# A fused sliding-window attention and GeGLU block on one core: the copy of the negated row maxima is issued in a later slot, and the last phase's weight loads and result stores are issued by GpSimd

## The chip, the cores and the metric

The kernel runs on one core of one Trainium2 chip. The metric is device time in microseconds (us) of one execution; the time of a kernel is the median of several executions. A profiled execution has a time of its own, and a span, which is the part of it that the hardware profiler recorded from the first instruction to the last.

The engines are called as in the profile: PE is TensorE's matmul, PEld its weight load, DVE is VectorE, ACT is ScalarE, POOL is GpSimd, SP is SyncE, which here does nothing but issue DMAs. "SPq" and "ACTq" are the queues from which SP and ACT issue DMAs; an issue is a short entry of such a queue, and the transfer itself runs later on the core's 16 DMA engines. Each engine takes its instructions in the order of the program; an instruction that waits holds up all that are behind it on the same engine. "L537" is line 537 of the kernel.

## The reference

One layer for 2048 tokens of width 640. The output is `x + attention(layernorm(x)) + geglu(layernorm(x))`, all in float32:

```python
qkv = xn @ wqkv                       # 32 heads of width 20
scores = q @ k.T * 20 ** -0.5         # a token sees itself and the 255 before it
p = softmax(where(0 <= i - j < 256, scores, -1e9))
attention = (p @ v) @ wo
geglu = (gelu(xn @ w_gate) * (xn @ w_up)) @ w_down      # inner width 1728
```

## The kernel before

**Number formats.** The dense products need more precision than one fast pass gives, so each float32 operand is split into a high part (a rounded copy, made by ACT) and a low part (the remainder, made by DVE or GpSimd), and each product is three matmuls: high by high, low by high, high by low. For the scores, q and k are split into three bf16 parts that are stacked along the partition axis, so that one matmul sums the products of parts.

**Stages.** Norm, transposes and the first projections come first (to about 102 us). Attention follows (102 to 541 us), with the remaining q, k and v projections and the first part of gate/up as filling for TensorE. Then the rest of gate/up (541 to 801 us), and last the down projection together with the attention's output projection (801 to 1041 us), which this text calls the last phase.

**Attention.** The work is cut into 32 units, u = 0 to 31; a unit is a group of 4 heads and a chunk of 512 tokens. `attention()` (L818) writes out the order of every engine's instructions by hand. A unit has a period of `NS` = 14 slots, and in each slot the loop puts down what is due: actions that were queued earlier for this slot (`at(slot, fn)`, `defer(n, fn)`, run by `tick()` at the start of a slot; those given to `late` are put down by `flush()` later in the same slot), then the fixed pieces, then dense matmuls as filling (`pull_fill`, 30.9 / 14 of them in each slot). In a period these matter here:

- *Stack loads.* `load_stack(u + 3)` brings q and k of a later unit from DRAM (qd, kd) into the stacked buffers qs and ks, by six DMAs each. SP issues the six of ks at the end of slot 9 (`KSLOT`) and the six of qs at the end of slot 12 (L473 to L482). There are several buffers of each, used in turn.
- *Row maxima.* In some slots `max_pair` makes scores of a later unit by matmul (L507) and DVE takes the maximum of each row (L517). The maxima are negated and, in slot 7 (`MXD`), `max_end(u)` (L531 to L537) turns them into rows: a matmul with the identity (L534), a copy by ACT into a small tile `mr` (L536), and a DMA issued by ACT (L537) that writes `mr` into rows 60 and 61 of the stacked buffer qs of unit u. That is "the row of negated maxima". The unit's score matmuls read these rows along with q, so that the maximum is subtracted inside the matmul.
- *Exponentials.* In the odd slots up to 11 of the unit's own period, which is the one after, `exp_piece` (L558) makes two banks of scores by matmul (L572) and ACT takes the exponential (L574). The first of these matmuls, in slot 1, is the first reader of the row. GpSimd masks the edges (L587, L590).
- *Outputs.* In slot 0 of the next period `av_unit` multiplies the exponentials by v (L615) and ACT copies the two results out (L621, L622); GpSimd adds them in slot 3, and SP stores them in slot 6 (L629, L630).
- *Projections.* `save_qk` splits a finished projection into the three bf16 parts `pt`, by ACT (L255), DVE and GpSimd (L259), and SP stores them to qd or kd (L268). Weights come by L234 and, for gate/up, by loads that ACT issues at some times.

All of SP's DMAs are one queue, in the order written. A DMA on one of the hardware queues also counts on one of a small set of completion semaphores, which the program's builder hands out in turn to SP's and ACT's DMAs alike; a DMA waits for the earlier one on its semaphore, even when that is one of another engine. So an issue can have to wait for a transfer that has nothing to do with its data.

**Last phase.** There are 80 steps: 8 passes p over 256 tokens each, and a pass has 9 steps of a quad of the inner width (two times 128 rows of the weight) and a tenth for the rest. In each step n of the loop:

- `load_step(n + 4)`: SP loads the activations of a step that is four later, into one of 5 buffers `hr`.
- `split_step(n + 2)`: ACT makes high parts (L1198), DVE low parts (L1077).
- `prepare(n)`: work on the weights, by the table `plan` (L1425): "f" fetches a quad's float32 weights into one of three staging buffers `stg` (`fetch`, L1031 to L1047, the DMA in L1043), "h" makes its high part on ACT (L1058), "l" its low part on DVE (L1062 and L1077), "s" forms sums of it on DVE. "b4" is the weight of quad 4, "t4" the sums of the same quad; the nine fetches in the table are b7, b8, t6, t8, t7, t0, t1, t2 and t3, in this order, in steps 4 to 12. They are issued by ACT (`eng=nc.scalar` in L1434). A fetch waits until its staging buffer has been read for the last time.
- `terms` (L1244): the matmuls, 128 x 320 each.
- `drain(p)` (L1262 to L1315), after a pass: DVE adds the accumulators into the tile `xr`, which holds x, and `store` (L1269 to L1271) writes its two halves to the output; SP issues these stores. `get_x` (L1317) loads x for the next pass into `xr`, in the fourth step of that pass.

After the table's fetches the weights are all in place, and the later passes only load activations.

Of the kernel before, what the change touches and what calls it, by code (L numbers as in the profile page):

```python
# [28 lines left out]
SR = 3 * DH  # L29
QROWS = 64 + SR  # L30
NS = 14
# [2 lines left out]
V1_SLOT = 169  # L34
MXD = 7
KSLOT = 9
LAG = 3, 5, 4, 4, 4, 4, 3, 3, 4, 3, 2, 1, 1, 1
NFA = 3
HD = D // 2
# [28 lines left out]
def block_kernel(ctx, tc, x, wqk, wv, wgu, wdo, wdl, out):  # L68
    nc = tc.nc
# [128 lines left out]
    now = [None]  # L198

    def at(slot, fn, *a):  # L200
        acts.setdefault(slot, []).append((fn, a))
# [3 lines left out]
    def late(fn, *a):  # L205
        if now[0] is None or now[0] < NS:
            fn(*a)
        else:
            lates.append((fn, a))

    def flush():
        while lates:
            fn, a = lates.pop(0)
            fn(*a)

    def lag():
        return 1 if now[0] is None or now[0] < NS else LAG[now[0] % NS]

# [119 lines left out]
    NQ, NK = 3, 4  # L338
    qs = [st1.tile([128, 4, C], BF, name=f"qs{i}") for i in range(NQ)]
# [133 lines left out]
    def load_stack(u, which=(0, 1)):  # L473
        g, c = divmod(u, NC)
        for m in range(80 * g // 128, (80 * g + 79) // 128 + 1):
            assert all((m + 5 * i, c) in done for i in which), (u, m)

        for i in which:
            dst, src, top, again = ((qs[u % NQ], qd[c], 1, 2), (ks[u % NK], kd[c], 0, 0))[i]
            for j in (0, 2):  # L480
                for p, part, n in ((j * 32, top, 2), (j * 32 + 2 * DH, again, 1), (64 - j * 32, 0, 3)):
                    nc.sync.dma_start(dst[p:p + DH * n, j:j + 2].rearrange("p j t -> p (j t)"),  # L482
                                      src[g, part:part + n].rearrange("s (d j) t -> (s d) (j t)",
                                                                      j=4)[:, j * C:(j + 2) * C])
# [46 lines left out]
    def max_end(u):  # L531
        nm = maxes.pop(u)
        ps = psm.tile([128, 128], F32, name="ps_n", tag="mx")
        nc.tensor.matmul(ps, nm.rearrange("p z a j b -> p (z a j b)"), identb, start=True, stop=True)  # L534
        mr = ap.tile([32, 128], BF, name="mr", tag="mr")
        nc.scalar.activation(mr, ps[0:32], AF.Copy)  # L536
        late(lambda: nc.scalar.dma_start(qs[u % NQ][SR:SR + 2].rearrange("p j t -> p (j t)"), mr))  # L537

    def pieces(c):
        b = 4 * c  # L540
# [259 lines left out]
    def pull_max(n, slot):  # L800
        for _ in range(n):
            x = next(stream, None)
            if x is None:
                return
            max_pair(*x)
            if x[1] == 7:
                at(slot + (MXD if slot >= 0 else 4), max_end, x[0])

    def tick():
        todo = [y for t in sorted(t for t in acts if t <= now[0]) for y in acts.pop(t)]  # L810
        return sorted(todo, key=lambda y: y[0] is max_end)

    def pull_fill(n):
        debt[0] += n
        while debt[0] > 0:
            debt[0] -= next(fill, 1.0)

    def attention():  # L818
# [22 lines left out]
        for u in range(NU + 1):  # L841
            for i in range(NS):
# [17 lines left out]
                flush()  # L860
                if u + 3 < NU and i in (KSLOT, 12):
                    load_stack(u + 3, (int(i == KSLOT),))
                pull_fill(RATE / NS)
# [164 lines left out]
    def four(t):  # L1028
        return t.rearrange("p k (h n) -> p (k h) n", h=2)

    def fetch(kind, q, where="stg", eng=nc.sync):  # L1031
        if where == "wr":
            ts = [wrp.tile([128, KT, 128], F32, name="wr", tag="wr").rearrange("p k m -> p (k m)") for _ in range(2)]
        elif where != "stg" and where != "at":
            ts = [tp.tile([128, D], F32, name=f"b{n}{q}", tag=f"x{n}{where}") for n in "hl"]
        if where != "stg" and where != "at":
            for i, t in enumerate(ts):
                nc.sync.dma_start(t, wdo[q][:, i])
            staged[kind, q] = [(t.rearrange("p (h n) -> p h n", h=2), slice(2 * i, 2 * i + 2)) for i, t in enumerate(ts)]
            return  # L1040
        pool, bufs = (rp3, 3) if where == "stg" else (cp, 3)
        t = pool.tile([128, 4, HD], F32, name="stg", tag=where, bufs=bufs)
        eng.dma_start(t, four(wdo[q]) if kind == "b" else wtd[q])  # L1043
        if kind == "t" and q in borrow:
            staged[kind, q] = [(t[:, i:i + 1], slice(i, i + 1)) for i in range(4)]
        else:
            staged[kind, q] = [(t, slice(0, 4))]  # L1047

    def parts(kind, q):
        for raw, dst in staged[kind, q]:  # L1050
            if kind == "t" and q in borrow:
                yield raw, quads["b", borrow[q] + dst.start], slice(1, 2)
            else:
                yield raw, slots(kind, q)[0][0], dst
# [15 lines left out]
    def sum_quad(q):  # L1070
        (t, _), = staged["b", q]
        for fn in sum_items(t):
            fn()
        staged["t", q] = [(t[:, i:i + 1], slice(i, i + 1)) for i in range(4)] if q in borrow else [(t, slice(0, 4))]

    def sub(o, i, j, op=OP.subtract):
        nc.vector.tensor_tensor(out=o, in0=i, in1=j, op=op)  # L1077
# [65 lines left out]
    NP = S // 256  # L1143
# [118 lines left out]
    def drain(p, ps, xt):  # L1262
        xs = {(r, h): xt[:, 2 - r, h * HD - HD:h * HD] for r in (1, 2) for h in (1, 2)}
        rows = {1: slice(256 * p + 128, 256 * p + 256), 2: slice(256 * p, 256 * p + 128)}

        def add(r, h, i, eng=nc.vector):
            eng.tensor_tensor(out=xs[r, h], in0=i, in1=xs[r, h], op=OP.add)  # L1267

        def store(r, h=None):  # L1269
            cs = slice(h * HD - HD, h * HD) if h else slice(0, D)  # L1270
            nc.sync.dma_start(out[rows[r], cs], xt[:, 2 - r, cs])  # L1271

        b = {i: ps[i][:, 0:HD] for i in ps}
        if p == 0:
            for bank, r, h in ((2, 1, 1), (3, 1, 2), (4, 2, 1), (8, 2, 2)):
                add(r, h, b[bank])
                if h == 2:
                    store(r)
            return
        a = copies.pop(p)  # L1280
        both = cp.tile([128, 2, HD], F32, name="u2", tag="r13")
        q, c5 = both[:, 0], both[:, 1]
        if p < NP - 1:
            nc.scalar.activation(c5, b[5], AF.Copy)
        if p == NP - 1:
            add(1, 1, b[2])
            add(1, 1, a)
            store(1, 1)
            sub(q, b[6], a, OP.add)
            add(1, 2, q)  # L1290
            sub(q, b[7], q, OP.add)
            add(2, 1, q)
            add(2, 2, q)
            add(2, 1, b[4])
            store(2, 1)
            add(1, 2, b[5])
            add(2, 2, b[5])
            store(2, 2)
            add(1, 2, b[3])
            store(1, 2)  # L1300
            return
        add(2, 1, b[4])
        sub(q, b[6], a, OP.add)
        add(1, 2, q)
        sub(q, b[7], q, OP.add)
        add(1, 2, b[3])
        add(1, 2, c5)
        add(1, 1, a)
        store(1)
        add(2, 1, q)  # L1310
        add(2, 2, c5)
        add(2, 2, q)
        if p == 1:
            add(2, 2, b[8])
        store(2)  # L1315
# [114 lines left out]
    def prepare(n):  # L1430
        for op in plan.get(n, "").split():
            kind, q = op[1], int(op[-1])
            if op[0] == "f":
                fetch(kind, q, eng=nc.scalar)  # L1434
            elif op[0] == "s":
                sum_quad(q)
            elif op[0] == "p":
                kind, q, i = "t", int(op[1]), int(op[2])
                for raw, t, dst in parts(kind, q):
                    raw, dst = (raw, dst) if q in borrow else (raw[:, i:i + 1], slice(i, i + 1))  # L1440
                    if q not in borrow or t is quads["b", borrow[q] + i]:
                        nc.scalar.activation(t[:, 0, dst], raw, AF.Copy)
                        sub(t[:, 1, dst], raw, t[:, 0, dst].bitcast(F32))
            else:
                (high_quad if op[0] == "h" else low_quad)(kind, q)
        if n == 2:
            nc.scalar.activation(w13[:, 0], raw13, AF.Copy)
            sub(w13[:, 1], raw13, w13[:, 0].bitcast(F32))
        if n == 0:
            fetch("b", 5)  # L1450
            fetch("b", 6)
# [76 lines left out]
```

## Time and profile before

| | |
|---|---|
| median of 3 executions | 1044.87 us (1044.46 to 1046.39) |
| the profiled execution | 1045.72 us |
| its span | 1044.0 us |
| instructions | 25563 |
| bytes moved by DMA | 158.74 MB, on average 152 GB/s |
| share of the 16 DMA engines' time, queue 1 (hardware) | 44.5% |

The span is 1.7 us shorter than the execution's own time; these lie around what is recorded.

How to read it: the page's first part gives for each engine its busy time, its share of the span and its number of instructions. The second part cuts the span into 40 slices of 26.1 us, with a digit for the busy share of each (9 is 90% or more):

```profile
ACT  4534766767666666666675322233224554433332
POOL 5122788888755787766461111101110000000000
...
DMA  5552356554633354343325576662216874433333
```

Counted from 0, slices 4 to 20 are attention: ACT and POOL are busiest there. From slice 31 on, which is the last phase, POOL has no work. There the DMA engines have their peak (8, then 7) in the slices that begin at 809 and 835 us, where the weights are fetched.

In the lists of groups, a row has the engine, the line, the operation and its tiles, a count and durations. In a timeline, a row is a start in us, a duration in us (for "x6" rows: from the first start to the last end of the six), the engine and the instruction, and in brackets how long the engine stood idle before it and which operation ended that. In a list of waits a row names the waiting line, what it waited for, and the total, number and longest of these waits.

### The profile page before, as it was taken

The numbers are of one execution on the slowest core, as the hardware profiler recorded it, in microseconds if no ns is written. First come the engines' busy times: TensorE is split into PE (matmuls) and PEld (weight loads), VectorE is DVE, ScalarE is ACT, GpSimd is POOL, SyncE is SP. The second block draws the span as 40 slices with busy tenths as digits, with TensorE's granted clock in tenths as the row PEclk, the third lists the DMA queues.
The fourth block names the chain that finished last, engine by engine and source line by source line (L and its number), as shares of the span: only waits on it lengthen the run. The fifth ranks groups of instructions, "written<-read, shape, count | busy, mean of one in ns | idle before, by whom it ended". The sixth has DMA issues, their size and how long they took to land.

```text
span 1044.0 us, 25563 instructions
## 1 busy us (share of the span) xinstructions
PE 1033.4 (99%) x9393; PEld 834.3 (80%) x9393; DVE 741.7 (71%) x2018; ACT 527.5 (51%) x1120; POOL 385.5 (37%) x623
## 2 busy tenths in 40 slices
PE   9999999999999999999999999999999999999998
PEld 8887666666777666666678888888888999999998
DVE  7755666677655676677736778776555889888887
ACT  4534766767666666666675322233224554433332
POOL 5122788888755787766461111101110000000000
PEclk9999999999999999999999999999999999999999
DMA  5552356554633354343325576662216874433333
GB/s 211 180 157 70 110 157 183 165 181 142 183 98 100 114 168 138 103 134 110 99 77 193 188 244 212 253 250 105 78 59 242 263 249 136 138 127 123 117 121 106
DMA packets 102150, 158.74 MB, mean 152 GB/s; under 512 B 14172, under 2 KB 55260, under 8 KB 102024
## 3 DMA queue, kind: packets, MB, share of 16 engines
q1 hardware_dynamic: 99640, 150.94, 44.5%
q10 hardware_dynamic: 2384, 6.16, 1.7%
q8 instruction: 74, 1.21, 0.5%
q14 instruction: 52, 0.43, 0.1%
HBM read 101.78 MB, written 54.92 MB: 150 GB/s over the span
## 4 chain that ended last, share of the span: by engine, by line
PE 90%; DVE 5%; ACT 2%; DMA 2%; issue 1%; POOL 0%; ACTq 0%; DVEq 0%; SPq 0%
PE ps_g L972 22%; PE ps_d L108 20%; PE ps L1244 20%; PE ps_e L572 8%; PE ps_v L108 7%; PE ps_o L615 5%; PE ps_m L507 5%; DVE junk L517 2%; PE ps_g L108 1%; DMA stg<-wdo 1%; ACT wb L1058 1%; PE ps_d L356 1%; PE ps_t L185 0%; DVE wb L1077 0%; DMA qs<-qd 0%
## 5 line engine op out<-in xcount | busy, mean ns | idle before, releaser
L517 DVE CUSTOM_DVE_ANT_0 junk<-ps_m,mask 128x320 bf16<-128x320 f32 (+2 forms) x512 | 243.0, 475 | 128.9 <-PE ps_m L507 71.0
L574 ACT ACTIVATE P<-ps_e 128x512 f32<-128x512 f32 (+2 forms) x384 | 198.7, 572 | 68.3 <-PE ps_e L572 67.8
L1244 PE MATMUL ps<-wb,at 128*128 128x320 f32 x999 | 156.4, 309 | 0.8 <-DVE xr L1267 0.8
L1244 PEld LDWEIGHTS ps<-wb,at 128*128 128x128 f32 x999 | 148.9, 188 | 1.5 <-issue 1.0
L587 POOL TENSOR_SCALAR_AFFINE_SELECT P<-P 128x256 f32<-128x256 f32 (+1 forms) x192 | 94.5, 494 | 73.2 <-ACT P L574 70.0
L572 PE MATMUL ps_e<-qs,ks 124*128 124x128 bf16 (+2 forms) x704 | 118.3, 278 | 0.1
L108 PE MATMUL ps_d<-xh,wqh 128*128 128x512 f32 x310 | 99.0, 422 | 0.2 <-ACT xh L193 0.2
L108 PE MATMUL ps_d<-xl,wqh 128*128 128x512 f32 x310 | 98.5, 422 | 0.0
L108 PE MATMUL ps_d<-xh,wql 128*128 128x512 f32 x310 | 97.6, 418 | 0.0
L101 POOL TENSOR_TENSOR wql<-wr,wqh 128x640 fp32r<-128x640 f32 x12 | 19.2, 1608 | 195.6 <-PE ps_g L972 171.1
L1244 PE MATMUL ps<-wt,at 128*128 128x320 f32 x552 | 88.9, 309 | 0.0
L572 PEld LDWEIGHTS <-ks 124*128 124x128 bf16 x704 | 49.5, 98 | 49.0 <-issue 33.4
L1244 PEld LDWEIGHTS ps<-wt,at 128*128 128x128 f32 x552 | 82.9, 188 | 0.1
L590 POOL TENSOR_SCALAR_AFFINE_SELECT P<-P 128x512 f32<-128x512 f32 (+1 forms) x144 | 76.7, 541 | 16.2 <-ACT P L574 16.2
L1198 ACT ACTIVATE at<-ss 128x512 fp32r<-128x512 f32 x59 | 37.3, 632 | 84.5 <-DVE ss L1077 84.5
L615 PE MATMUL ps_o<-P,v 64*32 64x320 f32 (+4 forms) x2816 | 74.2, 347 | 0.0
L259 POOL TENSOR_TENSOR pt<-r,pt 128x512 bf16<-128x512 f32 x40 | 46.8, 1169 | 64.6 <-ACT pt L255 57.0
L615 PEld LDWEIGHTS ps_o<-P,v 64*32 64x32 f32 x2816 | 50.8, 106 | 21.5 <-issue 0.9
L507 PE MATMUL ps_m<-ks,qs 60*64 60x320 bf16 (+3 forms) x1472 | 64.6, 260 | 3.4 <-DVE mx L517 1.5
L108 PEld LDWEIGHTS ps_d<-xh,wqh 128*128 128x128 f32 x310 | 56.0, 189 | 10.4 <-issue 1.6
L507 PEld LDWEIGHTS <-qs 60*64 60x64 bf16 x1472 | 29.1, 105 | 43.8 <-issue 35.6
L108 PEld LDWEIGHTS ps_d<-xh,wql 128*128 128x128 f32 x310 | 56.0, 189 | 10.1 <-issue 0.9
(195 smaller groups left out, 1967.4 us busy)
## 6 DMA issues: line engine op xcount, KB each, us to landing
hd<-he SPq DMA_DIRECT2D x50, 256.0 KB
hr<-hd SPq DMA_DIRECT2D x48, 256.0 KB
wr<-wgu SPq DMA_DIRECT2D x27, 320.0 KB
qs<-qd SPq DMA_DIRECT2D x64, 120.0 KB
ks<-kd SPq DMA_DIRECT2D x64, 120.0 KB
xi<-x SPq DMA_DIRECT2D x16, 320.0 KB
qs<-qd SPq DMA_DIRECT2D x64, 80.0 KB
ks<-kd SPq DMA_DIRECT2D x64, 80.0 KB
```

Of the source, the lines that this page charges most:

```text
L108: nc.tensor.matmul(ps, a(k), b(k), start=n == 0, stop=n == 3 * nk - 1)
L259: nc.gpsimd.tensor_tensor(out=pt[:, l, :], in0=r, in1=pt[:, 1, :], op=OP.subtract)
L507: nc.tensor.matmul(ps[64 * h:64 * h + 64, col:col + w], q[rows, j, q0:q0 + 64], ks_, start=True, stop=True, tile_position=(64 * r, 64 * h))
L517: nc.vector.tensor_tensor_reduce(out=junk[:, 0:n], in0=ps[:, 320 - n:320], in1=mask[:, 320 - n:320], scale=1.0, scalar=NEG, op0=OP.add, op ...
L572: nc.tensor.matmul(ps[:, col:col + n], k[0:QROWS, j, kc:kc + 128], q[0:QROWS, j, q0:q0 + n], start=True, stop=True)
L574: nc.scalar.activation(pt[:, j, lo:hi], ps[:, lo:hi], AF.Exp, scale=SCALE)
L587: nc.gpsimd.affine_select(out=a, in_=a, pattern=[[0, n], [1, 128]], compare_op=OP.is_ge, fill=0.0, base=0, channel_multiplier=-1)
L590: nc.gpsimd.affine_select(out=a, in_=a, pattern=[[0, n], [-1, 128]], compare_op=OP.is_ge, fill=0.0, base=-1, channel_multiplier=1)
L615: nc.tensor.matmul(os[r][32 * j:32 * j + 32, qa:qb], v[rows, w0_:w0_ + 32], pt[rows, j, col + qa - q0:col + qb - q0], start=r not in begun ...
L972: nc.tensor.matmul(ps, i, j, start=first and n == 0, stop=n == len(work) - 1, skip_group_check=True)
L1198: nc.scalar.activation(hi[:, 3:7], s, AF.Copy)
L1244: nc.tensor.matmul(ps[bank][:, 0:HD], *work[bank][j], start=bank not in begun, stop=final[p, bank] == n and j == len(work[bank]) - 1, skip ...
```

## The change

Three edits.

1. `max_end` no longer issues the DMA of the row of maxima in its own slot (7), but in slot 13 (`MRSLOT`) of the same period: it queues the issue with `at`, and the issue stays ACT's. The transposing matmul and the copy into `mr` stay in slot 7. Slot 13 is behind slot 9 and slot 12, at the ends of which SP is given the two stack loads of the period. Rows that are made before the first period (`now[0] < 0`) are issued at once.
2. The stores of the last phase's results are issued by GpSimd in place of SP, but for those of the last pass (p = 7).
3. The nine weight loads of the table in the last phase are issued by GpSimd in place of ACT.

```diff
@@ -34,6 +34,7 @@
 V1_SLOT = 169
 MXD = 7
 KSLOT = 9
+MRSLOT = 13
 LAG = 3, 5, 4, 4, 4, 4, 3, 3, 4, 3, 2, 1, 1, 1
@@ -534,7 +535,11 @@
         nc.tensor.matmul(ps, nm.rearrange("p z a j b -> p (z a j b)"), identb, start=True, stop=True)
         mr = ap.tile([32, 128], BF, name="mr", tag="mr")
         nc.scalar.activation(mr, ps[0:32], AF.Copy)
-        late(lambda: nc.scalar.dma_start(qs[u % NQ][SR:SR + 2].rearrange("p j t -> p (j t)"), mr))
+        issue = lambda: nc.scalar.dma_start(qs[u % NQ][SR:SR + 2].rearrange("p j t -> p (j t)"), mr)
+        if now[0] < 0:
+            issue()
+        else:
+            at(now[0] - now[0] % NS + MRSLOT, issue)
@@ -1268,7 +1273,7 @@
         def store(r, h=None):
             cs = slice(h * HD - HD, h * HD) if h else slice(0, D)
-            nc.sync.dma_start(out[rows[r], cs], xt[:, 2 - r, cs])
+            (nc.sync if p == NP - 1 else nc.gpsimd).dma_start(out[rows[r], cs], xt[:, 2 - r, cs])
@@ -1431,7 +1436,7 @@
             if op[0] == "f":
-                fetch(kind, q, eng=nc.scalar)
+                fetch(kind, q, eng=nc.gpsimd)
```

## The prediction

> **What bounds the kernel now.** I read the page first, then the busy time by stage, then who waits for whom, then the timeline at the two places that the waits point to.
>
> ```profile
> PE 1033.4 (99%) x9393; PEld 834.3 (80%) x9393; DVE 741.7 (71%) x2018; ACT 527.5 (51%) x1120; POOL 385.5 (37%) x623
> PE 90%; DVE 5%; ACT 2%; DMA 2%; issue 1%; POOL 0%; ACTq 0%; DVEq 0%; SPq 0%
> ...
> 102.00:541.00 439.00, 436.11 (x5847) 297.54 (x5842) 288.61 (x1068) 295.22 (x644) 321.83 (x547) 1.00 0.44 133
> 541.00:801.00 260.00, 260.00 (x1232) 214.74 (x1233) 179.34 (x296) 84.85 (x158) 31.33 (x24) 1.00 0.51 176
> 801.00:836.00 35.00, 34.19 (x231) 33.71 (x229) 29.40 (x38) 20.44 (x26) 0.00 (x0) 1.00 0.82 278
> 836.00:1041.00 205.00, 204.68 (x1391) 203.97 (x1391) 177.21 (x406) 80.75 (x155) 0.00 (x0) 1.00 0.42 140
> ```
>
> The first two lines are the page's busy times and its chain. The others are stages: attention, gate/up, the start of the last phase, its rest; the columns are length, then PE, PEld, DVE, ACT, POOL busy, clock, DMA share, GB/s. TensorE is busy everywhere, at full clock, so the change can only win what TensorE idles. In the last 205 us that is 205.00 - 204.68 = 0.32 us, in the 35 us before it 0.81 us, and in gate/up nothing. Attention leaves 2.9 us, and a little more behind modelled matmul ends.
>
> **Part 1, the row of maxima.** Moving its issue touches two things: what waits for the row, and what the row waits behind. First a row of SP's waits and one of TensorE's (us in total, times, longest), then the place of the latter in the timeline.
>
> ```profile
> SPq L482 <- DMA qs<-mr: 9.2, 6, 2.5
> ```
>
> ```profile
> PE ps_m L507 <- DMA qs<-qd: 0.6, 1, 0.6
> ```
>
> ```profile
> 153.78 0.62 ACTq L537 DMA_DIRECT2D qs<-mr  x1
> ...
> 153.32 4.27 SPq L482 DMA_DIRECT2D ks<-kd  x6
> ...
> 155.83 1.02 SPq L482 DMA_DIRECT2D ks<-kd  x3
> ...
> 158.61 1.34 SPq L268 DMA_DIRECT2D qd<-pt  x2
> 160.04 4.41 SPq L482 DMA_DIRECT2D qs<-qd  x6
> ...
> 165.64 0.27 PE L507 MATMUL ps_m<-ks,qs 60*64 60x256 bf16 x1
> 166.48 0.47 PE L507 MATMUL ps_m<-ks,qs 60*64 60x256 bf16 x15 [0.57 <-DMA qs<-qd]
> ```
>
> Six stack loads on SP stood still until a row of another unit had landed, 9.2 us in all. In this stretch the second key load was issued only at 155.83, 155.83 - 153.78 = 2.05 us after the row's issue on ACT; without it six issues of 1.02 / 3 = 0.34 us, as in the three from 155.83 on, would have been done by 153.32 + 2.0 = 155.4 instead of 157.59, so everything behind them on SP was 2 us late: weights, pt stores, the six query loads. The query loads ended so late that the max matmuls of 165.64 had to stop until 166.48: 0.84 us from start to start. In the list of waits it is TensorE's only one for a stack load; the other five waits of SP ended far ahead of the loads' first readers. With the row issued six slots later the key loads no longer stand behind it. **I take -0.84 us**; the ends are -0.84 and 0 (0 if the pt store at 158.61, which waits for GpSimd, holds the query loads anyway).
>
> What the move adds: the row must land before the next unit's first exp matmul, which reads it. One period, SP, ACT and PE:
>
> ```profile
> 258.15 2.44 SPq L482 DMA_DIRECT2D ks<-kd  x6
> 260.69 2.16 SPq L482 DMA_DIRECT2D qs<-qd  x6
> ...
> 257.56 1.09 ACT L574 ACTIVATE P<-ps_e 128x512 f32<-128x512 f32 x2 [0.46 <-PE ps_e L572]
> 258.53 0.63 ACT L255 ACTIVATE pt<-r 128x512 bf16<-128x512 f32 x1
> 261.92 0.60 ACT L621 ACTIVATE ob<-ps_o 128x512 f32<-128x512 f32 x1 [2.75 <-PE ps_o L615]
> ...
> 263.04 0.34 PE L572 MATMUL ps_e<-qs,ks 124*128 124x384 bf16 x1
> ```
>
> ```profile
> L537 ACTq EVENT_SEMAPHORE  x32: 17/17/17, 81.3 to 523.2; - x32
> ...
> 268.29 0.62 ACTq L537 DMA_DIRECT2D qs<-mr  x1
> ...
> 272.88 1.78 SPq L482 DMA_DIRECT2D ks<-kd  x5
> ```
>
> ACT's last work ahead of slot 13 is the pt copy that ends at 259.16; then it idles 2.75 us until the first attention output. The issue of 0.62 us fits into that idle time, and it leaves 263.04 - 259.16 = 3.9 us for landing. A row took 2.05 us above, and 4.6 us (268.29 to 272.88) when it was issued right behind two gate/up weight loads. Stack loads lie between: I take 2.5 us, and the row is in time. ACT's own wait before the issue was 17 ns in all 32 cases, so I cost the new place at 0. Queued behind it on ACT are the output copies L621 and L622, which wait for TensorE until 261.9. On SP, what now may wait for the row is eight issues later: pt stores and the od stores of the next period, which nobody reads soon. GpSimd's queue is not passed in this stage.
>
> **Part 2, nine weight loads from ACT to GpSimd.** The last phase's hold of 0.81 us, and the ACT and DVE rows that lead to it:
>
> ```profile
> 827.05 1.74 ACTq L1043 DMA_DIRECT2D stg<-wtd  x2
> 828.84 1.27 ACT L1058 ACTIVATE wb<-stg 128x1280 fp32r<-128x1280 f32 x1 [1.99 <-DVE wt L1077]
> ...
> 831.67 0.33 ACTq L1043 DMA_DIRECT2D stg<-wtd  x1
> 832.04 1.27 ACT L1058 ACTIVATE wt<-stg 128x1280 fp32r<-128x1280 f32 x1 [1.41 <-DMA stg<-wtd]
> ...
> 825.53 1.49 DVE L1077 TENSOR_TENSOR wb<-stg,wb 128x1280 fp32r<-128x1280 f32 x1
> 830.14 1.49 DVE L1077 TENSOR_TENSOR wb<-stg,wb 128x1280 fp32r<-128x1280 f32 x1 [1.12 <-ACT wb L1058]
> 833.35 1.49 DVE L1077 TENSOR_TENSOR wt<-stg,wt 128x1280 fp32r<-128x1280 f32 x1 [1.11 <-ACT wt L1058]
> 834.75 0.68 DVE L1077 TENSOR_TENSOR at<-hr,at 128x512 fp32r<-128x512 f32 x1
> 835.36 1.68 DVE L1267 TENSOR_TENSOR xr<-ps,xr 128x320 f32<-128x320 f32 x4
> ...
> 835.99 1.70 PE L1244 MATMUL ps<-wb,at 128*128 128x320 f32 x10 [0.81 <-DVE xr L1267]
> ```
>
> TensorE waits at 835.99 for the first pass's accumulators to be added out (L1267), which stands in DVE's order behind the low part of "ft6" (833.35), which waits for its high part on ACT (832.04). ACT stands still twice because a load that it is to issue waits for a staging buffer: 1.99 us before 828.84, and the issue at 831.67. Those stops go. But the copy at 832.04 also waited for its data: its load was issued at 827.05, when DVE gave the buffer back (825.53 + 1.49), and landed about 831.7, 4.7 us later, with the DMA engines 0.82 busy. So the chain is now set by this landing: the copy moves by **D - 0.3 us**, where D is what an issue by GpSimd takes beyond one by ACT, and 0.3 is 832.04 less 831.7. The load of "fb7" before it (high part done at 824.7, low part begun at 825.53) has 0.8 us in hand; beyond that it delays the buffer, and the shift is 2D - 1.1. The gain can't exceed the hold of 0.81.
>
> D isn't in this trace: GpSimd issues no DMA. The nearest rows:
>
> ```profile
> L1043 ACTq DMA_DIRECT2D stg<-wtd x7: 326/327/340, 827.1 to 845.5; - x7
> ...
> L259 POOL TENSOR_TENSOR pt<-r,pt 128x512 bf16<-128x512 f32 x40 | 46.8, 1169 | 64.6 <-ACT pt L255 57.0
> ```
>
> Below, D = -0.33 (an issue that costs nothing); above, D = 1.17 - 0.33 = 0.84 (as long as GpSimd's slowest frequent instruction). I take 0.4, nearer to the short issues (ACT's 0.33 and 0.62). Then the hold changes by +0.1 us; ends -0.6 and +0.6.
>
> [...]
>
> **Part 3, 14 result stores from SP to GpSimd** (seven passes; the last pass stays on SP, so the tail is unchanged).
>
> ```profile
> SPq L1271 <- DVE xr L1267: 100.0, 12, 12.5
> ```
>
> SP stood 100 us in front of these stores, with the hr loads of later steps behind it. Yet TensorE lost 0.32 us in this whole stretch, because loads are issued four steps ahead, 4 x 21 matmuls x 0.147 us (205.00 / 1391) = 12.3 us. The gain is nothing (at most 0.3). A later landing costs nothing either: xr is loaded again at step 3 and first read at step 9, 18 us later. GpSimd has no other work here (0.00 busy), so stores that wait for DVE block only later fetches; the ones behind the first pass's stores ("ft1" to "ft3") are used from step 13 on.
>
> **Sum**, against the profiled execution: 1045.72 us, of which 1044.0 is the span and 1.72 lies around it. -0.84 + 0.1 + 0 = -0.74, giving 1044.98; against the median of 1044.87 the same step gives **1044.1 us**. Ends of the unknowns: -0.84 - 0.6 = -1.4 (1043.4) and 0 + 0.6 (1045.5).
>
> **Rivals.**
> - *Nothing moves* (0.10): SP's wait for the row is replaced by another, GpSimd's D just eats ACT's freed time: 1044.9.
> - *Stack loads matter more than I think* (0.10). LDWEIGHTS shows short waits that end with DMAs:
>
> ```profile
> PEld L507 <- issue: 35.6, 110, 0.5
> ...
> PEld L507 <- DMA od<-ob: 2.0, 6, 0.4
> PEld L507 <- DMA kd<-pt: 1.8, 5, 0.4
> ```
>
> If these are true waits for loads that SP issues late, they and 0.84 go: -4.6, 1040.3. Against it: at 0.33 us each they are as long as the 110 that wait for nothing.
> [...]
> - *The row comes late* (0.08): its issue gets behind both stack loads on the way to the DMA engines, or ACT has to wait for one of them to land first. From the last query load's issue (262.85) plus 2.05 it lands at 264.9, 1.9 us after 263.04, and TensorE, which takes its work in order, stops. In the eleven periods up to 277 us (counted in SP's timeline), where SP is as full as here, at most 11 x 1.9 = 21 us, with half of it given back since a longer period leaves SP more time: +10, 1055.
>
> **How the numbers follow.** The forecast has 0.58. A measurement of this kernel can tell about 0.2%, 2.1 us, from no change: below 1042.8 is faster, above 1047.0 slower. Faster: the second rival and 0.08 of the forecast, if the gains of both parts come at full size with one that I don't see: 0.18. Slower: the late loads 0.13, the late row 0.08: 0.21. The rest, 0.61, is no difference. The range leaves out the late row and the second rival: 1042.4 to 1048.3, which takes in D up to 2.7.
>
> **What would show it.** Right: no wait of L482 for qs<-mr, the stop near 165.6 gone, the row's issue after the period's last exp copies and ACT's idle time before L621 as before, the hold near 836 within 0.6 us of 0.8. Wrong: TensorE or ACT waiting at a period's start for qs<-mr; ACT's L1058 idle behind stg loads by more than 2 us; a hold in step 8 or 9 of the last phase.

## The result and the profile after

The changed kernel is slower: 1052.48 us (median of 6, 1049.94 to 1056.92) beside 1045.28 us for the kernel before, run along with it; the ratio is 1.0069 with a 95% interval of 1.0051 to 1.0088, some 7.2 us. The prediction was 1044.1 us, with a range up to 1048.3. The profiled execution took 1054.47 us, its span is 1052.7 us against 1044.0. The ratios in this text leave out two executions that took about twice as long or more, one of the kernel before (2020.9 us) and one of the kernel with the row issued by GpSimd in slot 8 (2568.1 us), for which the record has no cause.

Edits moved the line numbers by up to 5: L507 is L508 now, L537 is L538, L572 is L577, L1244 is L1249. First the page's busy times and the engines' part of its chain, after:

```profile
PE 1036.9 (98%) x9393; PEld 836.2 (79%) x9393; DVE 742.0 (70%) x2018; ACT 526.9 (50%) x1120; POOL 397.7 (38%) x646
PE 88%; DVE 5%; DMA 2%; ACT 2%; issue 1%; POOL 0%; DVEq 0%; SPq 0%; ACTq 0%
```

TensorE does the same 9393 matmuls and is busy 3.5 us longer for them; the rest of the loss is idle time. That the same work takes longer points to the clock; its rows follow below. The same four stretches of both kernels, before and then after (length, then PE, PEld, DVE, ACT, POOL busy, granted clock, DMA share, GB/s):

```profile
102.00:320.00 218.00, 216.82 (x3001) 149.84 (x2989) 144.36 (x548) 147.77 (x333) 171.48 (x290) 1.00 0.50 150
320.00:541.00 221.00, 219.29 (x2848) 147.70 (x2853) 144.25 (x520) 147.44 (x312) 150.35 (x258) 1.00 0.37 116
```

```profile
102.00:320.00 218.00, 212.60 (x2853) 145.57 (x2844) 139.89 (x528) 142.88 (x317) 165.08 (x279) 0.98 0.50 146
320.00:541.00 221.00, 219.32 (x2952) 148.73 (x2951) 148.19 (x539) 145.62 (x315) 150.83 (x259) 1.00 0.40 117
```

Between 102 and 320 us TensorE got through 2853 matmuls where it did 3001 before, idled 4.2 us more (216.82 - 212.60) and had a clock of 0.98. From 320 us on it is as before. By the start of the last phase nearly all of the loss is there: the same matmul begins at 805.77 before and at 813.75 after, 7.98 of the 8.7 us between the spans.

```profile
805.77 10.57 PE L1244 MATMUL ps<-wb,at 128*128 128x320 f32 x71
```

```profile
813.75 10.58 PE L1249 MATMUL ps<-wb,at 128*128 128x320 f32 x71
```

Lined up matmul by matmul, the two traces come apart in two places: by 3.95 us between 163 and 169 us, and by 3.73 us between 221 and 230 us (times of the kernel before). Here is the first, in PE's timeline after:

```profile
162.59 0.39 PE L577 MATMUL ps_e<-qs,ks 124*128 124x128 bf16 x2
...
167.48 0.27 PE L508 MATMUL ps_m<-ks,qs 60*64 60x256 bf16 x1 [1.70 <-DMA qs<-qd]
168.92 0.47 PE L508 MATMUL ps_m<-ks,qs 60*64 60x256 bf16 x15 [1.18 <-DMA qs<-qd]
```

It is the very stop for the query loads that the prediction wanted to see gone, 0.57 us of idle time before and 1.70 + 1.18 = 2.88 us now. And behind it the clock drops to a half (windows of PE after, granted clock third from the end):

```profile
165.80:169.40 3.60, 0.74 (x17) 0.49 (x18) 0.81 (x2) 1.57 (x3) 2.06 (x4) 1.00 0.81 257
169.40:170.40 1.00, 1.00 (x5) 0.85 (x6) 0.85 (x4) 0.49 (x1) 0.47 (x1) 0.51 0.55 187
170.40:171.40 1.00, 1.00 (x4) 0.69 (x3) 0.71 (x5) 1.00 (x3) 0.00 (x0) 0.50 0.25 57
171.40:172.40 1.00, 1.00 (x6) 0.47 (x5) 0.32 (x2) 0.34 (x2) 0.80 (x1) 0.50 0.67 174
172.40:173.40 1.00, 1.00 (x6) 0.86 (x5) 0.00 (x0) 0.84 (x3) 0.35 (x1) 0.78 0.08 31
```

At a half, a stretch costs half its length: 0.49 + 0.50 + 0.50 + 0.22 = 1.71 us. With 2.88 - 0.57 = 2.31 us more idle time that makes 4.0 us, the 3.95 that the traces came apart. The second place is alike, 0.91 and 1.01 us of stop and the same slow clock behind it, 0.50 for 3.41 us:

```profile
228.19 0.27 PE L508 MATMUL ps_m<-ks,qs 60*64 60x256 bf16 x1 [0.91 <-DMA qs<-qd]
229.46 0.47 PE L508 MATMUL ps_m<-ks,qs 60*64 60x256 bf16 x15 [1.01 <-DMA qs<-qd]
```

Why were the query loads late? SP's waits for the row, after (us in total, times, longest):

```profile
SPq L483 <- DMA qs<-mr: 24.9, 13, 3.3
...
SPq L235 <- DMA qs<-mr: 2.7, 1, 2.7
SPq L696 <- DMA qs<-mr: 2.6, 1, 2.6
...
SPq L269 <- DMA qs<-mr: 2.3, 1, 2.3
...
SPq L762 <- DMA qs<-mr: 1.0, 1, 1.0
```

They were 9.2 us in 6 waits; they are 33.5 us in 17, and 13 of them are waits of the stack loads themselves. ACT and SP at the first place:

```profile
158.26 0.62 ACTq L538 DMA_DIRECT2D qs<-mr  x1
```

```profile
154.83 2.58 SPq L483 DMA_DIRECT2D ks<-kd  x6
160.15 1.58 SPq L235 DMA_DIRECT2D wr<-wqk  x2
161.83 1.33 SPq L269 DMA_DIRECT2D qd<-pt  x2
163.26 2.46 SPq L483 DMA_DIRECT2D qs<-qd  x6
```

The key loads do go out in one run now (2.58 us; 4.27 before). But SP is done with them at 157.41 and then stands for 2.7 us, until 160.15: the weight load that is next counts on the row's semaphore, ACT issues the row only at 158.26, and it lands 1.9 us later. (In the trace after, SP's 982 and ACT's 32 DMAs count on eight semaphores in a fixed turn, and this weight load is eight DMAs behind the row; GpSimd's 23 count on eight others.) So the last of the six query loads is issued at 165.7, 1.3 us later than before. They are slower too: the chain of waits has one that took 3.8 us from 164.98 on. The weight loads, now later as well, are just ahead of it; that they are the cause isn't shown.

```profile
164.98 3.80 DMA qs<-qd
```

At the second place it is the key loads that stand: SP's longest wait for the row, 3.3 us, is among them, for a row that ACT issues at 219.75. The six took 2.34 us before.

```profile
219.28 5.55 SPq L483 DMA_DIRECT2D ks<-kd  x6
```

### The profile page after: what moved, and what is told of

The parts are those of the page before. It is cut to its first block, busy times and chain, and to the rows that moved or that the text cites. A ratio compares the mean times of both kernels' runs of the same rounds, so it can differ in the third digit from the quotient of the medians.

```text
span 1052.7 us, 25578 instructions
## 1 busy us (share of the span) xinstructions
PE 1036.9 (98%) x9393; PEld 836.2 (79%) x9393; DVE 742.0 (70%) x2018; ACT 526.9 (50%) x1120; POOL 397.7 (38%) x646
## 4 chain that ended last, share of the span: by engine, by line
PE 88%; DVE 5%; DMA 2%; ACT 2%; issue 1%; POOL 0%; DVEq 0%; SPq 0%; ACTq 0%
PE ps_g L977 22%; PE ps_d L109 20%; PE ps L1249 19%; PE ps_e L577 8%; PE ps_v L109 6%; PE ps_o L620 5%; PE ps_m L508 5%; DVE junk L518 2%; PE ps_g L109 1%; DMA stg<-wdo 1%; DMA qs<-qd 1%; PE ps_d L357 1%; PE ps_t L186 0%; DVE xr L1272 0%; ACT wb L1063 0%
## 5 line engine op out<-in xcount | busy, mean ns | idle before, releaser
L1249 PE MATMUL ps<-wb,at 128*128 128x320 f32 x999 | 156.4, 309 | 1.2 <-DVE xr L1272 1.0
L1249 PEld LDWEIGHTS ps<-wb,at 128*128 128x128 f32 x999 | 148.9, 188 | 1.9 <-issue 1.3
L577 PE MATMUL ps_e<-qs,ks 124*128 124x128 bf16 (+2 forms) x704 | 119.5, 280 | 0.1
L577 PEld LDWEIGHTS <-ks 124*128 124x128 bf16 x704 | 50.0, 99 | 49.1 <-issue 32.4
L1249 PE MATMUL ps<-wt,at 128*128 128x320 f32 x552 | 88.9, 309 | 0.0
L1249 PEld LDWEIGHTS ps<-wt,at 128*128 128x128 f32 x552 | 82.9, 188 | 0.1
L508 PE MATMUL ps_m<-ks,qs 60*64 60x320 bf16 (+3 forms) x1472 | 65.0, 260 | 7.7 <-DMA qs<-qd 4.8
L1276 POOL DMA_DIRECT2D out<-xr x14 | 7.6, 544 | 165.8 <-DVE xr L1272 160.5
L508 PEld LDWEIGHTS <-qs 60*64 60x64 bf16 x1472 | 29.3, 105 | 48.7 <-issue 35.5
```

Of the source, the lines that this page charges most:

```text
L508: nc.tensor.matmul(ps[64 * h:64 * h + 64, col:col + w], q[rows, j, q0:q0 + 64], ks_, start=True, stop=True, tile_position=(64 * r, 64 * h))
L577: nc.tensor.matmul(ps[:, col:col + n], k[0:QROWS, j, kc:kc + 128], q[0:QROWS, j, q0:q0 + n], start=True, stop=True)
L1249: nc.tensor.matmul(ps[bank][:, 0:HD], *work[bank][j], start=bank not in begun, stop=final[p, bank] == n and j == len(work[bank]) - 1, skip ...
```

## The experiments

The theory to be tested (A): the row, issued late by ACT, holds up SP, which shares its semaphores, in front of the query loads; in two periods in which SP has no time to spare TensorE stops for them, and the clock behind the stops costs 1.7 us again, as at 169.4 us. Against it: the row comes too late for its own reader (B); the loss is GpSimd's in the last phase (C). Each ratio is to runs of the kernel before on the same chip, with its 95% interval.

**The first edit alone.** The change, without its last two hunks.

> Only the first edit: the row of maxima is issued by ACT in slot 13; the last phase's DMAs stay with SP and ACT. Theory A (SP stands behind the row): a DMA of SP that comes eight places behind the row in the list of DMAs waits until the row has landed; where the six query loads are behind it, the max matmuls stop for about 2 us and the clock halves for 3 to 4 us after it, some 4 us each time. Then this kernel has nearly the whole loss: ratio 1.006 to 1.008 (6 to 8.5 us), SP's waits for qs<-mr at 25 us or more, TensorE's waits for qs<-qd at 3 us or more. Theory B (the row is late for its own reader): the same ratio, but TensorE's stops are in the score matmuls behind exp, released by qs<-mr. Theory C (the loss is GpSimd's in the last phase): ratio 0.999 to 1.001.

Measured: 1.0080 (1.0062 to 1.0098). The first edit has all of the loss. SP's waits for the row are 28.8 us in 18, TensorE's waits are 4.4 us for qs<-qd and none for qs<-mr: A, not B or C.

**The last phase alone.** The change, with the row issued where it was:

```diff
-        if now[0] < 0:
-            issue()
-        else:
-            at(now[0] - now[0] % NS + MRSLOT, issue)
+        late(issue)
```

> Only the second and third edits: the nine weight loads and the stores of seven passes are issued by GpSimd; the row of maxima stays in slot 7. Theory A: 0 to +0.8 us (ratio 1.000 to 1.001), the hold of the first drain 0.8 to 1.1 us. Theory B: the same. Theory C: +6 us or more (ratio 1.006).

Measured: 1.0001 (0.9992 to 1.0009): nothing, for nine loads and fourteen stores. C falls.

**The row in slot 13, from SP.** The first edit alone, with

```diff
-        issue = lambda: nc.scalar.dma_start(qs[u % NQ][SR:SR + 2]...
+        issue = lambda: nc.sync.dma_start(qs[u % NQ][SR:SR + 2]...
```

> The row in slot 13 as in the change, but issued by SP in place of ACT, so that it stands in SP's own order and not ahead of it; last phase as before. Theory A: SP has eight issues of its own between the row and the one that waits for it, about 3 us, so the waits of SP for qs<-mr fall to under 5 us in total and TensorE's stops for qs<-qd don't exceed 1 us: ratio 0.999 to 1.001. Theory B: the row is issued still later than by ACT, so TensorE waits for it at the beginning of many periods: ratio 1.006 or more.

Measured: 1.0187 (1.0164 to 1.0211), far from the expectation of A. Half of that expectation held: TensorE has no stop for qs<-qd any more. But B's stops appear instead. TensorE's wait, then SP's row and the score matmul that waits for it:

```profile
PE ps_e L577 <- DMA qs<-mr: 14.5, 15, 3.2
```

```profile
223.25 2.15 SPq L483 DMA_DIRECT2D qs<-qd  x6
225.50 0.69 SPq L538 DMA_DIRECT2D qs<-mr  x1
```

```profile
227.82 0.39 PE L577 MATMUL ps_e<-qs,ks 124*128 124x128 bf16 x2 [3.18 <-DMA qs<-mr]
```

"Behind both stack loads" in SP's own queue is too late for the reader; ACT's queue, which runs ahead at that point, had the row in time.

**The row in slot 13, from GpSimd.** As above, with nc.gpsimd.

> The row in slot 13, issued by GpSimd in place of ACT; last phase as before. GpSimd's DMAs count on semaphores of their own, so no DMA of SP can wait for the row. Theory A: SP has no wait for qs<-mr, TensorE's stops for qs<-qd fall to 1 us or less; ratio 0.999 to 1.001, unless GpSimd's masks make the row late for its reader, which would show as stops in the score matmuls. Theory B: stops in the score matmuls released by qs<-mr, as in the change: ratio 1.006 or more.

Measured: 1.0246 (1.0229 to 1.0263). SP never waits for the row, and there is no stop for qs<-qd, but GpSimd's masks are ahead of the row and it is late for its reader: stops of 10.1 us at L577. A cost that neither theory had comes on top: 9.8 us in four stops of max_end's matmul, which waits for DVE. DVE was held in a single short instruction, the negation of the maxima. Its median is 0.18 us in this run, and its longest in the kernel before is 0.99 us; four times here it took 3.88 to 5.55 us and ended within 0.05 us of the end of an unbroken run of GpSimd's instructions. What in GpSimd's work holds it isn't shown. One of the four, and the last of GpSimd's run:

```profile
186.56 5.47 DVE L527 TENSOR_SCALAR nm<-mx 128x16 bf16<-128x16 f32 x1
```

```profile
190.79 1.22 POOL L595 TENSOR_SCALAR_AFFINE_SELECT P<-P 128x512 f32<-128x512 f32 x2
```

Both runs say that A's wait and B's lateness are two costs of the same slot, and which one is paid depends on whose queue the row is in.

**The row in slot 10, from ACT.** The first edit alone with `MRSLOT = 10`.

> The row in slot 10, issued by ACT, two slots' worth earlier than in the change; last phase as before. Theory A (a DMA of SP that counts on the row's semaphore stands until the row has landed, so the query loads behind it come late): the row is issued about 2 us later than in slot 7, the key loads stand by so much longer, and at least one stop of TensorE for qs<-qd over 1.5 us with a halved clock behind it remains: ratio 1.002 to 1.008. Theory D (only a row behind the stack loads is bad, because it lands late or delays the next period): 0.999 to 1.001.

Measured: 1.0012 (1.0000 to 1.0023), less than A expected and hardly more than D did; by itself this run doesn't tell the two apart. SP's waits for the row are 17.4 us in 11, twice those of before, yet TensorE has no stop for qs<-qd in the profiled execution. The query loads of the first place show why: they are out by 160.91 + 3.25 = 164.2, where the change had 165.7.

```profile
160.91 3.25 SPq L483 DMA_DIRECT2D qs<-qd  x6
```

So a wait of SP costs nothing up to a limit, and the limit lies within those 1.5 us. The other profiles narrow it down: with the six out by 163.1 to 163.8 there is no stop here (the two further profiles of the kernel before, the last phase alone, the row from GpSimd in slot 8), and with 160.04 + 4.41 = 164.45, in the profile that the prediction read, there is one of 0.57 us.

**The row in slot 8, from SP and from GpSimd.** As the two runs in slot 13, with `MRSLOT = 8`.

> The row in slot 8, issued by SP ahead of the key loads; last phase as before. No other engine's issue time is in SP's queue any more, and the row is five slots earlier than where SP had it in the run before. Theory A: no stop of TensorE for qs<-qd or qs<-mr; ratio 0.9985 to 1.000 (the stop of 0.84 us of the kernel before is gone). Theory B (an issue by SP as such makes the row late): stops at qs<-mr as in that run, ratio over 1.005.

Measured: 1.0017 (1.0004 to 1.0030), slightly slower, against the expectation. There is no stop for the row; there is one of 0.63 us for qs<-qd near 222 us and one of 1.3 us near 798 us, in the gate/up stage (L977, for DVE's L980). What this second one has to do with the row, if anything, stays open.

> The row in slot 8, issued by GpSimd, on semaphores that SP doesn't share; last phase as before. Theory A: SP has no wait for qs<-mr, TensorE no stop over 1 us for a stack load; ratio 0.9985 to 1.001. Theory B (an issue by GpSimd as such makes the row late, behind its masks): stops at qs<-mr, ratio over 1.005.

Measured: 1.0001 (0.9989 to 1.0013), as A expected: no wait of SP for the row, no stop of TensorE for a stack load or for the row. The row as such, on GpSimd's queue and early, costs nothing; what cost in slot 13 was the slot.

**More work for SP, without the row.** The kernel before, with six tiny loads ahead of the query loads of each period, into tiles that nobody reads; and the same with three.

```diff
+    spare = [st1.tile([1, 8], F32, name=f"spare{i}") for i in range(6)]
...
+        if which == (0,):
+            for t in spare:
+                nc.sync.dma_start(t, x[0:1, 0:8])
         for i in which:
```

> The kernel before, but with six loads of 32 bytes each, into spare tiles that nobody reads, issued by SP ahead of the six query loads of each period: about 2 us more for SP, with the row in slot 7. It doubles the suspected cost without the row. Theory A (late query loads are what costs): stops of TensorE for qs<-qd of 1.5 to 2.5 us in the periods in which SP is full, near 165 and 222 us at least, each with a clock of about a half for 3 us behind it, some 4 us each: ratio 1.003 to 1.012. Theory E (SP's delay is absorbed, the row itself is the cause): 0.999 to 1.001.

> As the run with six more loads on SP ahead of the query loads, with three of them, about 1 us a period. Theory A with a threshold: a delay of 1 us lengthens stops that exist and makes few that reach 2 us: ratio 1.001 to 1.006. If the cost were proportional to the delay, half of the other run's 1.0116: 1.0058.

Measured: 1.0116 (1.0100 to 1.0131) with six, 1.0038 (1.0023 to 1.0052) with three. TensorE's waits with six, and the stop at the first place with three:

```profile
PE ps_m L512 <- DMA qs<-qd: 8.5, 8, 2.0
```

```profile
167.32 0.47 PE L512 MATMUL ps_m<-ks,qs 60*64 60x256 bf16 x15 [1.45 <-DMA qs<-qd]
```

The row is in slot 7 here, and the stops begin with those of the change, at the same place: the query loads are out by 165.7 with three and 167.0 with six. That query loads which SP issues later cost several us is shown without the row. With six, only the stop of 1.97 + 0.97 us at the first place halved the clock (0.50 from 170 to 173 us); the others, 0.93 to 1.55 us, cost their length (the clock was 1.00 from 246 to 250 us, behind one of them). The added loads also take semaphores in turn and so change who waits for whom, but SP's waits for the row are only 12.2 us in 11 with six. Three cost a third of what six cost, not half. With three, the longest stop of the profiled execution was 1.45 us and its granted clock 1.0; but that was the fastest of twelve (1046.22 us, median 1049.72), and in nine of the others the granted clock was 0.998 or less.

**Slot 13 from ACT, with less work for SP.** The first edit alone; besides, GpSimd issues the loads of the projections' weights during attention.

```diff
-        nc.sync.dma_start(raw, wqk[t])
+        (nc.gpsimd if now[0] is not None and now[0] >= 0 else nc.sync).dma_start(raw, wqk[t])
...
-            nc.sync.dma_start(raw, wv[h, :, k, :])
+            (nc.gpsimd if now[0] is not None and now[0] >= 0 else nc.sync).dma_start(raw, wv[h, :, k, :])
```

> The row in slot 13, issued by ACT as in the change; besides, the loads of the projections' weights (two or three in a period, wr and wvr) are issued by GpSimd instead of SP while attention runs; last phase as before. Theory A (the loss is SP's lateness at the query loads in the two or three periods in which SP is full): SP gains about 1 us in a full period, and near 160 us no weight load stands behind the row any more, so TensorE's stops for qs<-qd fall under 1 us each and the clock isn't halved: ratio 0.999 to 1.002; more only if TensorE's stops are released by GpSimd's own work. Theory F (a row in slot 13 costs 6 us whatever SP has to do): ratio 1.006 to 1.009.

Measured: 1.0063 (1.0040 to 1.0086): A's number is missed, and F's is met, for a reason that neither had. The stops for qs<-qd did fall under 1 us each (1.5 us in 3). But two weight loads of 320 KB go out just as the row is issued, and the row stands among them:

```profile
157.90 1.09 POOL L235 DMA_DIRECT2D wr<-wqk  x2
```

```profile
158.13 0.62 ACTq L538 DMA_DIRECT2D qs<-mr  x1
```

```profile
164.46 0.61 PE L577 MATMUL ps_e<-qs,ks 124*128 124x128 bf16 x2 [1.92 <-DMA qs<-mr]
```

Here the row takes 6.3 us to its reader and TensorE stops for it, 1.92 us, with the halved clock behind it (0.50 from 164 to 167 us). In slot 13 the row has little to spare on its own side as well.

**The kernel before, profiled twice more.** Unchanged.

> The kernel before, unchanged, profiled anew: do the two stops on which the sum rested, 0.84 us near 166 us (qs<-qd) and 0.81 us near 836 us (L1267), belong to the kernel or to that one execution? If to the kernel: both are there within 0.2 us, and the profiled time is 1045.5 to 1046. If to the execution: one or both are missing and the time is shorter by what is missing, 1043.6 to 1045.

> The kernel before a third time, same question: both stops there and 1045.5 to 1046, or one or both missing and a time that is shorter by them.

Measured: 1044.2 and 1043.78 us, and neither stop is there in either. The first of the two, SP and TensorE near 166 us and TensorE in the last phase:

```profile
160.23 3.54 SPq L482 DMA_DIRECT2D qs<-qd  x6
```

```profile
165.78 0.75 PE L507 MATMUL ps_m<-ks,qs 60*64 60x256 bf16 x16
...
821.77 27.15 PE L1244 MATMUL ps<-wb,at 128*128 128x320 f32 x184
```

The sixteen max matmuls run through, and so do 184 matmuls across the place where 0.81 us were lost. So the two stops on which the sum rested, 0.84 and 0.81 us, don't belong to every execution: without them the kernel took 1.5 and 1.9 us less than the 1045.72 us of the execution that had been profiled. How much of them is in the median execution, which lies between (1045.3 us), isn't known.

## Why the prediction was wrong

**The step that failed** is "on SP, what now may wait for the row is eight issues later: pt stores and the od stores of the next period, which nobody reads soon". It took the order of the slots for the order in which the semaphores are handed out. By the row's new slot, eight places behind it lie such stores. In the program as built, the row was listed further forward, ahead of the query loads or among the key loads in most periods, though ACT comes to it last: for the 32 rows, the DMA eight places behind was 16 times a stack load (5 of keys, 11 of queries), twice a weight load and only 12 times a store (of the last two rows it was none of these). The runs showed 17 waits of 33.5 us where 6 of 9.2 us had been, and 13 of the 17 at stack loads; the prediction's first sign of being right was that there would be none. Nor were the key loads free of the row, as the prediction took them to be: at the second place they stood 3.3 us for it. In the list of the kernel before, 26 of the 32 rows had a stack load eight places behind. So it is not the number of loads that may wait which grew, but how long SP stands there until ACT gets to its issue. The trace of before had the warning: the waits of L482 were already for a row that SP's list had overtaken, SP being at slot 9's loads (153.32) while ACT was still in slot 7 (153.78). Issue the row later and SP meets it again.

**-0.84 us for the stop at 165.64.** Wrong twice. The stop isn't in two other profiles of the kernel before, so it could not be counted on in the median. And the stop meant something else: that in this period the query loads have no time to spare. The same row could have been read as the price list of a further delay. It was read as a gain.

**The price of a stop.** The prediction priced a stop at its length. The runs showed that the clock can come on top: at the first place 2.31 us of more idle time and 1.71 us by the clock, about 4 us. Most of the loss is the stops themselves, though: the one execution of the change whose granted clock was 1.0 took 1049.94 us, still 4.7 us more than the median of before; the other five, with 0.998 to 0.995, took 1050.86 to 1056.92 us.

**The row is in time for its reader** (2.5 us taken). Right for the change as it is: 1.9 us from 158.26 to 160.15, the reader at 162.59, no stop for qs<-mr, and ACT's wait before the issue was 17 ns as before. But the margin was thin, as the three runs show in which the row was late.

**The weight loads from GpSimd.** D was taken as 0.4 us, the hold to grow by 0.1 us (-0.6 to +0.6). DVE, GpSimd, ACT and PE after, for the load of "ft6":

```profile
834.42 1.49 DVE L1082 TENSOR_TENSOR wb<-stg,wb 128x1280 fp32r<-128x1280 f32 x1
```

```profile
836.20 0.53 POOL L1048 DMA_DIRECT2D stg<-wtd  x1 [3.78 <-DVE wb L1082]
```

```profile
840.54 1.27 ACT L1063 ACTIVATE wt<-stg 128x1280 fp32r<-128x1280 f32 x1 [2.09 <-DMA stg<-wtd]
```

```profile
844.49 11.82 PE L1249 MATMUL ps<-wb,at 128*128 128x320 f32 x79 [1.05 <-DVE xr L1272]
```

From the buffer's release (835.91) to the copy it takes 4.63 us; before, 832.04 - 827.02 = 5.0 us, or 4.7 to the estimated landing. So D was about zero here: GpSimd's issue begins 0.3 us after the release and takes 0.53 us, and the landing is no later. The hold is 1.05 us against 0.81, inside the range. That the whole edit is worth nothing is shown by the run of the last phase alone; the hold comes and goes without it. The prediction's chance of late loads, 0.13, and the D of up to 2.7 in its range have no run behind them: in the 14 us from 836 on DVE was busy 11.56 us, and each of GpSimd's issues took 0.53 to 0.55 us.

**The stores.** Nothing, as predicted. SP now waits for them in another way, the loads of x (L1324) for GpSimd's stores to land, 33.5 us in 7 waits, and those loads have the time.

**The rivals.** "Nothing moves" had the mechanism (SP's wait is replaced by another) with a price of nothing. "The row comes late" had a time, 1055, near the one measured, but by a mechanism that shows only where SP or GpSimd issues the row, or where weight loads go out beside it. The chance of a loss over 0.2% was put at 0.21.

What stays open: why the stops differ so much between executions of one kernel (1049.9 to 1056.9 us), how much of the loss is due to the slower query transfers at the first place rather than to their later issue, and the stop near 798 us of the run with the row from SP in slot 8. Nothing tried beats the kernel before beyond its interval; the row from GpSimd in slot 8 and the last phase alone equal it.

## What to carry to other kernels

Before a DMA is issued later, ask which DMA of another queue waits on the same semaphore, from the list as built and not from the slots, and what stands behind that one. A stop that the profile shows on a tight resource is evidence of no slack there before it is a gain to collect, and one profile doesn't say that it is in the next execution: profile the unchanged kernel twice before counting on tenths of a microsecond. Before pricing a stop of TensorE by its length, read the granted clock behind it: here it was 0.50 for 3.41 us behind stops of 0.91 + 1.01 us and 1.00 behind one of 2.02 us.

## What the runs showed of the hardware

- **The clock after a stop.** Between 100 us and the last matmuls the change has two stretches of 3.41 us at a granted clock of 0.50, about 1.7 us lost in each. TensorE had idled 3.41 - 0.76 = 2.65 us of the 3.41 us ahead of the first, in the stops of 1.70 and 1.18 us, and 3.41 - 1.67 = 1.74 us of those ahead of the second, in those of 0.91 and 1.01 us (length, PE busy and so on, granted clock third from the end):

```profile
166.01:169.42 3.41, 0.76 (x17) 0.51 (x18) 0.83 (x2) 1.57 (x3) 1.87 (x4) 1.00 0.83 263
169.42:172.83 3.41, 3.41 (x14) 2.37 (x14) 1.86 (x8) 2.10 (x5) 1.60 (x2) 0.50 0.45 130
...
227.45:230.86 3.41, 1.67 (x23) 1.29 (x24) 0.89 (x3) 0.57 (x2) 1.51 (x3) 1.00 0.76 232
230.86:234.27 3.41, 3.41 (x12) 1.94 (x10) 1.11 (x6) 2.98 (x8) 1.93 (x3) 0.50 0.20 62
```

  In the run with the row from SP in slot 13 the stop of 3.18 us was followed by the lower clock, 0.53 on average over 3.5 us, and one of 2.10 - 0.08 = 2.02 us by none:

```profile
224.60:227.90 3.30, 0.12 (x3) 0.08 (x3) 1.64 (x8) 0.00 (x0) 1.26 (x2) 1.00 0.61 165
227.90:231.40 3.50, 3.50 (x13) 2.34 (x14) 0.69 (x1) 2.22 (x5) 0.00 (x0) 0.53 0.58 174
...
274.90:277.00 2.10, 0.08 (x3) 0.06 (x2) 1.74 (x9) 0.32 (x1) 1.34 (x2) 1.00 0.46 137
277.00:280.50 3.50, 3.50 (x32) 2.27 (x33) 0.89 (x3) 1.95 (x5) 0.94 (x2) 1.00 0.57 168
```

  So the length of a single stop doesn't give its price here. What decides it was not tested.
- **A small DMA behind large ones.** The same row landed 1.9 us after its issue in the change and reached its reader 6.3 us after it when 2 x 320 KB had been issued by GpSimd beside it.
- **DMAs issued by GpSimd** took it 0.53 to 0.55 us each in the last phase (0.70 us the first), and 0.61 us in attention, where the row landed 1.9 to 4.7 us after its issue (slot 8, from GpSimd):

```profile
L538 POOL DMA_DIRECT2D qs<-mr x32: 610/610/742, 82.2 to 524.1; - x32
...
DMA to landing us min/median/max: 1.9/2.7/4.7
```
